# Tiles padded to multiples of 64 bytes, and a planner told of shorter input loads, in a fused recurrence and expert kernel

## The chip, the cores and the metric

The kernel runs on one core of one Trainium2 chip. The metric is the device time of one execution in microseconds (us). The kernel before takes 300.28 us, median of 3 runs (300.28 to 300.85). The change is small against that, so the spread matters here more than usual: in other sessions the same kernel gave single runs from 299.97 to 302.95 us, and every comparison below is with runs of the kernel before from the same session. Ratios are the mean time of one kernel's fast runs over the mean of the other's fast runs in the same rounds, so they are not quite the ratio of the medians that I quote. Brackets behind a ratio hold its 95% interval.

## The reference, cut to what matters

```python
# first stage: gated linear recurrence, B=4, H=8, S=768, D=48
f = 1 / (1 + exp(-f_logit))
for t in range(S):
    state = f[:, :, t, :, None] * state + einsum('bhd,bhe->bhde', k[:, :, t], v[:, :, t])
    y[:, :, t] = einsum('bhd,bhde->bhe', q[:, :, t], state)
# second stage: four experts on x = y as (3072, 384); w1 (4, 384, 1024), w2 (4, 1024, 384)
p = domain_probs / (domain_probs.sum(-1, keepdims=True) + 1e-9)
for e in range(4):
    out += p[:, e:e+1] * (maximum(x @ w1[e], 0) @ w2[e])
```

The recurrence is computed in 6 chunks of 128 steps, as small attention; each chunk's y goes through the four experts. TensorE spends most of its time in the experts.

## The kernel before

Nothing in the program fixes the order of instructions by hand. A planner simulates the engines with a table of costs, and the instructions are then emitted in the order in which its steps began. A load of one batch (128 rows of time, 8 heads of 48 floats: 192 KB in runs of 192 bytes) costs 1.1 us in chunk 0 and 1.05 us later:

```python
def add_load(c, nm, b, n, prio, deps=(), cost=None):
    op = P.add(f"ld {nm}{c}.{b}", {"DMA": cost or (1.05 if c else 1.1) * n}, lambda e: load(c, nm, b, n), prio,
               deps=deps, takes=[(nm, c, b // 2)], lag=2.0)
    ...
for i, x in enumerate("f0 k0 q0 f1 k1 q1 f2 f3 k2 q2 v0 k3 q3 v1 v2 v3".split()):
    add_load(0, x[0], int(x[1]), 1, -1000 + i)
add_load(1, "f", 0, 1, -980, cost=0.1)
...
def load_w(i, e, which, ks, cols):          # expert weights, issued by GpSimd
    ins["w", i] = nc.gpsimd.dma_start(out=w[:, e, ks, cols], in_=r[e][:, ks, cols])
    if i == 0:
        after(ins["w", 0], ins[0, "q", B - 1])      # not before the last q of chunk 0
```

Some tiles are short. They push all that is allocated behind them off a multiple of 64 bytes:

```python
ones = const.tile([T, 1], BF16)             # takes 32 bytes of each partition
...
ident32 = const.tile([NR, NR], FP32)        # NR = 24: 96 bytes
psm = const.tile([T, NR], FP32)             # 96 bytes
shapes = { ... "egs": ([128, NP], FP32), ...}   # 16 bytes
```

Where the plan leaves TensorE waiting before the first expert matmul, the program fills the time with matmuls on a dummy tile (`busy`), 34 of them. One gate step of a later chunk is the chain that will matter: ScalarE reads f (`ex = exp(-f)`, then `gp = ln(1 + ex)`), TensorE sums `gp` along time (line 268), ScalarE takes exponentials of that, GpSimd multiplies q and k by them.

## Time and profile before

| what | kernel before |
|---|---|
| time, median | 300.28 us |
| span in the profile | 298.3 us |
| last q of chunk 0 lands | 16.51 us |
| first / second weight lands | 22.78 / 24.69 us |
| first expert matmul / first on the second weight | 22.83 / 24.73 us |
| from 25.4 us on | TensorE busy without a gap |

The landing times are read from the trace's records of each transfer's last landing. The prediction below shows the page, the stretches and the chain of waits. Three more views are needed for the comparison. Busy time by stretches, in the stretch of the input loads and in the one after the weights' issue; the figures in order are stretch, length, busy time of PE, PEld, DVE, ACT and POOL, granted clock, the DMA engines' share by their packets' time, and GB/s:

```profile
4.00:16.00 12.00, 9.73 (x94) 5.21 (x92) 7.24 (x13) 8.96 (x22) 3.48 (x3) 1.00 1.36 196
...
17.00:18.00 1.00, 0.93 (x10) 0.61 (x8) 1.00 (x3) 0.98 (x4) 1.00 (x2) 1.00 1.35 199
```

The page's row for the queue of all loads that SyncE issues (packets, MB, share of the span that its packets took):

```profile
q1 hardware_dynamic: 129348, 30.14, 60.2%
```

And what TensorE waited for from 14 to 26 us (in total, times, longest):

```profile
PE ps_m L364 <- DMA w_sb<-in_moe_w_dram: 1.1, 2, 0.8
PE ps_t L335 <- DVE vb L228: 0.8, 1, 0.8
PE ps_t L360 <- ACT yb L226: 0.5, 1, 0.5
```

The two waits of line 364 are for the first weight and for the second. The second is the one that counts: after it TensorE never stops again.

### The profile page before, as it was taken

How to read it: one execution, taken by the hardware profiler on the slowest of the kernel's cores; microseconds unless marked ns; L12 is line 12 of the kernel's file. 1: busy time of each engine (PE TensorE's matmuls, PEld its weight loads, DVE VectorE, ACT ScalarE, POOL GpSimd, SP SyncE). 2: the span in 40 equal slices, each digit the busy share in tenths (PEclk: the TensorE clock that was granted, in tenths of full speed). 3: DMA queues.
4: the chain of work that ended last, by engine and by line, in shares of the span. 5: the costliest groups of instructions: out<-in, count | busy, mean ns of one | idle time of the engine just before them, and what ended most of it. 6: DMA issues, size and time to landing. Idle time of an engine off the chain costs nothing.

```text
span 298.3 us, 5572 instructions
## 1 busy us (share of the span) xinstructions
PE 289.1 (97%) x2160; PEld 170.6 (57%) x2160; DVE 126.1 (42%) x247; ACT 176.5 (59%) x325; POOL 105.7 (35%) x179
## 2 busy tenths in 40 slices
PE   6879999999999999999999999999999999999995
PEld 2447555567777776455555555555555555555553
DVE  6657003585675584036375444332532322201223
ACT  4776673857775687877464674555465544465440
POOL 5377401329389159325547553234220000000000
PEclk9999999999999999999999999999999999999999
DMA  8999999997999999999999962102431100200003
GB/s 146 197 186 202 208 208 185 192 186 181 167 165 154 219 156 178 204 185 152 196 168 194 205 115 35 29 0 62 110 69 38 26 2 26 79 2 0 0 0 108
DMA packets 136462, 36.82 MB, mean 123 GB/s; under 512 B 126812, under 2 KB 135644, under 8 KB 136436
## 3 DMA queue, kind: packets, MB, share of 16 engines
q1 hardware_dynamic: 129348, 30.14, 60.2%
q0 software_dynamic: 7088, 6.33, 13.6%
q8 instruction: 17, 0.28, 0.4%
q14 instruction: 9, 0.07, 0.1%
HBM read 31.51 MB, written 4.72 MB: 121 GB/s over the span
## 4 chain that ended last, share of the span: by engine, by line
PE 91%; DMA 4%; SPq 4%; issue 0%; POOL 0%; DVE 0%
PE ps_m L379 42%; PE ps_m L364 42%; SPq L232 3%; DMA w_sb<-in_moe_w_dram 2%; PE ps_t L320 2%; DMA q<-in_q_dram 1%; PE ps_t L335 1%; PE ps_t L331 1%; PE ps_t L341 1%; PE ps_t L268 1%; SPq L247 0%; POOL w_sb L239 0%; PE ps_t L305 0%; DVE o L386 0%; PE ps_t L360 0%
## 5 line engine op out<-in xcount | busy, mean ns | idle before, releaser
L375 ACT ACTIVATE h<-ps_m 128x512 bf16<-128x512 f32 (+1 forms) x192 | 102.5, 538 | 91.1 <-PE ps_m L364 87.5
L364 PE MATMUL ps_m<-xT,w_sb 128*128 128x512 bf16 (+1 forms) x696 | 152.1, 342 | 1.1 <-DMA w_sb<-in_moe_w_dram 1.1
L379 PE MATMUL ps_m<-w_sb,h 128*128 128x384 bf16 (+1 forms) x776 | 151.6, 324 | 0.0
L379 PEld LDWEIGHTS <-h 128*128 128x128 bf16 x776 | 75.1, 98 | 58.6
L386 DVE SCALAR_TENSOR_TENSOR o<-ps_m,pn,o 128x384 f32<-128x384 f32 (+1 forms) x73 | 44.7, 612 | 110.6 <-PE ps_m L379 104.3
L364 PEld LDWEIGHTS <-w_sb 128*128 128x128 bf16 x696 | 65.5, 98 | 43.9 <-DMA w_sb<-in_moe_w_dram 1.5
L296 POOL TENSOR_TENSOR qk<-q,e 128x384 bf16<-128x384 f32 x19 | 22.5, 1191 | 33.9 <-ACT e L288 22.3
L324 DVE TENSOR_TENSOR AT<-ps_t,mask 128x512 bf16<-128x512 f32 x48 | 29.9, 681 | 5.4 <-PE ps_t L320 5.4
L355 POOL TENSOR_TENSOR Sf<-Sf,egs 48x192 f32<-48x192 f32 x40 | 20.1, 503 | 30.8 <-DVE Sf L348 28.7
L288 ACT ACTIVATE e<-ps_t 128x384 f32<-128x384 f32 x48 | 26.6, 668 | 4.0 <-PE ps_t L268 2.9
L373 DVE TENSOR_SCALAR h<-ps_m 128x256 bf16<-128x256 f32 (+1 forms) x40 | 20.0, 510 | 18.9 <-PE ps_m L364 16.6
L296 POOL TENSOR_TENSOR qk<-k,e 128x384 bf16<-128x384 f32 x20 | 20.3, 1018 | 8.4 <-ACT egs L290 4.7
L348 DVE TENSOR_TENSOR Sf<-Sf,ps_t 48x192 f32<-48x192 f32 x40 | 14.0, 350 | 10.9 <-PE ps_t L341 10.2
L239 POOL DMA_DIRECT2D w_sb<-in_moe_w_dram x11 | 9.0, 823 | 21.0 <-DMA k<-in_k_dram 17.6
L356 POOL CAST sb<-Sf 48x192 bf16<-48x192 f32 x40 | 13.6, 340 | 2.6
L388 ACT ACTIVATE o<-ps_m,pn 128x384 f32<-128x384 f32 x22 | 12.8, 581 | 2.8 <-PE ps_m L379 1.7
L228 POOL CAST vb<-v 128x384 bf16<-128x384 f32 x18 | 9.7, 557 | 9.9 <-DMA v<-in_v_dram 6.0
L260 ACT ACTIVATE ex<-f 128x768 f32<-128x768 f32 (+1 forms) x14 | 10.5, 747 | 3.9 <-DMA f<-in_f_logit_dram 3.9
L614 PE MATMUL ps_m<-busy 128*128 128x512 bf16 x34 | 10.9, 424 | 1.5 <-DVE busy L144 1.5
L293 POOL DMA_DIRECT2D egs<-e x16 | 9.0, 565 | 9.4 <-ACT e L288 9.4
L335 PE MATMUL ps_t<-vb,AT 128*128 128x48 bf16 x192 | 11.5, 184 | 0.9 <-DVE vb L228 0.8
L226 ACT CAST yb<-ps_t 128x384 bf16<-128x384 f32 (+1 forms) x16 | 7.6, 472 | 7.5 <-PE ps_t L335 7.3
(54 smaller groups left out, 122.9 us busy)
## 6 DMA issues: line engine op xcount, KB each, us to landing
out_dram<-o SPq DMA_DIRECT2D x23, 192.0 KB, 2.0
w_sb<-in_moe_w_dram POOLq DMA_DIRECT2D x5, 768.0 KB, 18.2
k<-in_k_dram SPq DMA_DIRECT2D x10, 384.0 KB, 5.3
q<-in_q_dram SPq DMA_DIRECT2D x10, 384.0 KB, 6.2
v<-in_v_dram SPq DMA_DIRECT2D x10, 384.0 KB, 6.1
f<-in_f_logit_dram SPq DMA_DIRECT2D x9, 384.0 KB, 5.0
w_sb<-in_moe_w_dram POOLq DMA_DIRECT2D x6, 384.0 KB, 8.7
f<-in_f_logit_dram SPq DMA_DIRECT2D x6, 192.0 KB, 4.5
```

Source lines behind the costliest of these rows:

```text
L288: nc.scalar.activation(out=o, in_=i, func=AF.Exp, scale=1.0 if j else -1.0)
L296: engines[eng].tensor_tensor(out=tl("qk", c, b)[:, j, :, 0:D].rearrange("t (i r) d -> t i r d", r=2), in0=tl("qk"[j], c, b // 2)[:, hh(b), ...
L324: nc.vector.tensor_tensor(out=tl("AT", c, b)[:, r].rearrange("s i t -> s (i t)"), in0=tl("A", c, b, r).rearrange("s i t -> s (i t)"), in1= ...
L335: nc.tensor.matmul(out=y[:, h * D:(h + 1) * D], lhsT=AT[:, r, i, :], rhs=vb[:, h, :], start=(c == 0), stop=True, skip_group_check=True)
L348: nc.vector.tensor_tensor(out=Sf[rows, b], in0=Sf[rows, b], in1=KV[rows, :, r, :], op=ALU.add)
L355: nc.gpsimd.tensor_tensor(out=Sf[rows, b], in0=Sf[rows, b], in1=eg, op=ALU.mult)
L356: nc.gpsimd.tensor_copy(out=nb[rows, b, :, r * D:(r + 1) * D], in_=Sf[rows, b])
L364: nc.tensor.matmul(out=tl("hp", c, e, fc, n0)[:, n0:n1], lhsT=w1_sb[:, e, kk, fc * 128:(fc + 1) * 128], rhs=tl("xT", c)[:, kk, n0:n1], sta ...
L373: nc.vector.tensor_relu(out=dst, in_=src)
L375: nc.scalar.activation(out=dst, in_=src, func=AF.Relu)
L379: nc.tensor.matmul(out=tl("op", c, e, nt, part)[:, cols], lhsT=tl("h", c, e, half_of(c, nt * T))[:, fc, nt * T:(nt + 1) * T], rhs=w2_sb[:, ...
L386: nc.vector.scalar_tensor_tensor(out=o, in0=op, scalar=pe, in1=o, op0=ALU.mult, op1=ALU.add)
```

## The change

Each short tile is made a multiple of 64 bytes (the padding isn't used), so that every tile starts at one; and since loads are expected to become shorter, the planner is told so, by 14% in chunk 0 and 5% later.

```diff
-    ones = const.tile([T, 1], BF16)
+    ones = const.tile([T, 32], BF16, name="ones")[:, 0:1]
-    ident32 = const.tile([NR, NR], FP32)
+    ident32 = const.tile([NR, 32], FP32, name="ident32")[:, 0:NR]
-    psm = const.tile([T, NR], FP32)
+    psm = const.tile([T, 32], FP32, name="psm")[:, 0:NR]
-        "ex": ([T, 2 * H, D], FP32), "egs": ([128, NP], FP32), ...
+        "ex": ([T, 2 * H, D], FP32), "egs": ([128, 16], FP32), ...
 (three uses of egs take [:, 0:NP]: cut)
-        op = P.add(f"ld {nm}{c}.{b}", {"DMA": cost or (1.05 if c else 1.1) * n}, ...
+        op = P.add(f"ld {nm}{c}.{b}", {"DMA": cost or (1.0 if c else 0.95) * n}, ...
```

So there are two changes in one: where the data lie, and the order of the instructions. Padding alone leaves the order on every engine as it was; the costs alone give the order of the changed kernel. Between the two orders, apart from 4 dummies, only five instructions change their engine by the two traces (one relu, one scaling of an output, one copy, and one product each of q and k, which change places).

> **What bounds the kernel now.** I read the page first, then busy time by stretches, then the chain that ended last, then the timeline of the first 27 us. The page:
>
> ```profile
> span 298.3 us, 5572 instructions
> PE 289.1 (97%) x2160; PEld 170.6 (57%) x2160; DVE 126.1 (42%) x247; ACT 176.5 (59%) x325; POOL 105.7 (35%) x179
> PE   6879999999999999999999999999999999999995
> DMA  8999999997999999999999962102431100200003
> L614 PE MATMUL ps_m<-busy 128*128 128x512 bf16 x34 | 10.9, 424 | 1.5 <-DVE busy L144 1.5
> ```
>
> TensorE is busy 97% of the span, but 10.9 us of that are matmuls on a dummy tile (line 614), which the planner puts where it expects TensorE to wait. All of them lie before the first expert matmul, so the first slices are far less full than they look. I then cut the span where the first expert matmul starts and where the dense part begins:
>
> ```profile
> 10.00:22.80 12.80, 10.31 (x128) 6.24 (x128) 8.43 (x16) 9.66 (x22) 8.08 (x10) 1.00 1.32 189
> 22.80:25.40 2.60, 2.32 (x26) 1.89 (x27) 1.59 (x6) 1.39 (x5) 1.57 (x3) 1.00 1.23 201
> 25.40:295.30 269.90, 269.85 (x1976) 159.79 (x1972) 109.91 (x208) 160.21 (x288) 91.67 (x152) 1.00 0.70 118
> ```
>
> The first pair of figures in each row is stretch and length; the next is PE's busy time. From 25.4 to 295.3 us PE has 269.85 of 269.90 us. Is that real work or a stretched wait? The chain of waits shows groups of 3 matmuls of line 364 at 0.65 us and groups of 4 of line 379 at 0.65 us. There are 6 chunks x 4 experts x (8 + 8) such groups = 384, and 384 x 0.65 = 249.6 us; the chain gives these two lines 42% + 42% of 298.3 = about 249 us. So the experts run at the rate of one group's own time, and the middle has nothing to give. What is left is 22.8 us at the front and 3 us at the end. What holds the front:
>
> ```profile
> 10.12 0.52 ACT L260 ACTIVATE ex<-f 128x384 f32<-128x384 f32 x1 [0.42 <-DMA f<-in_f_logit_dram]
> ...
> 15.55 0.56 DVE L296 TENSOR_TENSOR qk<-k,e 128x384 bf16<-128x384 f32 x1 [0.83 <-DMA k<-in_k_dram]
> ...
> 16.80 7.15 POOL L239 DMA_DIRECT2D w_sb<-in_moe_w_dram  x9 [2.42 <-DMA q<-in_q_dram]
> ...
> 20.31 0.51 ACT L226 CAST vb<-v 128x384 bf16<-128x384 f32 x1 [1.11 <-DMA v<-in_v_dram]
> ...
> 22.83 1.16 PE L364 MATMUL ps_m<-xT,w_sb 128*128 128x256 bf16 x9 [0.82 <-DMA w_sb<-in_moe_w_dram]
> ```
>
> The brackets name what each engine sat idle for: loads, all the way. The first weight may be issued only when the last q has landed (16.5 us), and the first expert matmul waits for that weight. The rate of the DMA engines from 3 to 22.8 us sets when the dense part begins.
>
> **What the Trainium skill says.** "DMA: Bandwidth & Descriptors", section Specifications, wants at least 512 B for line rate. The trace agrees: the input loads are 192 B packets (48 floats), and 192 KB land every 1.05 us or so, about 187 GB/s; the weight pieces (2 KB read, 1 KB written per row) land every 1.92 us for 768 KB read, about 410 GB/s. The same page, section Queues, rings and completion order, says each DMA engine goes round its queues packet by packet. The trace agrees: once the weights are issued at 16.8 us, a v load takes 1.88 us from the landing before it in place of 1.05, so loads and the first weight share one rate, and shortening loads brings the weight forward. "SBUF — State Buffer", section Operand start alignment, says only that an operand must start at a multiple of its element size, and that its runs timed nothing: no page there says what a tile's start at a multiple of 32 but not of 64 costs a DMA. For that I need the trace.
>
> **The change part by part.** (1) Alignment. In the built program before, a 2-byte tile that takes 32 bytes (`ones`) moves all that follows to an odd multiple of 32; further small tiles move it again. Of the input tiles that the first chunk loads into (f0, k0, q0, f1, k1, q1, v0, v1), one alone, f1, happens to start at a multiple of 64 (byte 130304); f2, for the first load of chunk 1, doesn't. The change puts every tile at a multiple of 64. So the kernel before holds the experiment already. The trace's landing records, in us from each load's last landing to that of the next, in the order of issue: k 1.14, q 1.07, f 1.03, k 1.06, q 1.02, **f 0.91, f 0.92**, k 1.05, q 1.05, v 1.28 (a small load of probabilities shares it), k 1.05, q 1.05. The two in bold are the two halves of f1. Same size, same shape, same queue, same queue depth: 0.13 us less, 13%. That is also the 14% that the planner is told (1.10 to 0.95). Rows step by 192 B, so from any base at a multiple of 64 they run through the same four places within 256 B; f1's 256 B base should be no better than the new 64 B ones.
>
> (2) What this is worth. Before the first weight lands at 22.78 us, 17 loads land (16 of chunk 0 and the first of chunk 1); 2 are fast already. 15 x 0.13 = **1.95 us**. The last q comes 11 x 0.13 = 1.4 us earlier (about 15.1), and the first weight about 20.8 us. I give weights and stores no gain: their runs are 1 KB and longer, and they are hidden after that.
>
> (3) The planner. The order of instructions, compared engine by engine, shows the same matmuls of real work in another order and 30 dummy matmuls for 34. Dummies lie in the wait, so 4 x 0.42 us are no gain by themselves. The last batch's y matmuls (0.36 us) and its three transposes (0.33) matter: before, y stood ahead of the first expert matmul; now three expert groups stand ahead of it. So when the second weight lands, 1.9 us after the first in either kernel, some 0.33 us more is still to do. That comes off: 1.95 - 0.33 = **1.6 us**.
>
> (4) Can the other engines follow? From 9 to 21 us VectorE has 2.8 us of idle time, of which 0.83 and 1.12 wait for k and v themselves; ScalarE waits 0.61, 0.70 and 1.11. The waits for loads shrink when loads are earlier, and the rest of the chain moves with them. It is tight: VectorE's last two mask products (1.28 us) now end near 20, and y follows; but y no longer stands ahead of the first expert matmul, so a lag of some tenths is covered.
>
> (5) The middle. 4.8% shorter costs for later loads reorder stores, transposes and a few evictions (one relu from DVE to ACT, one first output scaling the other way). PE has work at every moment there; later data earlier saves nothing.
>
> Sum: 300.28 - 1.6 = **298.7 us**; in the profile the span goes from 298.3 to about 296.7.
>
> **The rivals.** *The start becomes bound by VectorE and ScalarE.* For: ScalarE has 4.21 of 5 us busy from 10 to 15, VectorE 3.84. Against: both still name loads as what they wait for. It would halve the gain: 299.5. *Alignment pays beyond the loads, and the new order closes the small gaps of the front too.* For: from 22.8 to 25.4 PE has 0.28 us idle, and weights move too. Against: the second weight remains a wait. It would make 298.0. *The new order opens a hole later.* For: the stretch from 60 to 120 us mixes attention and experts, and a planner with wrong costs can order an engine badly; DMA is 90% busy there. Against: before, PE lost nothing there, with costs no better. A missed wait would cost 1 to 2 us and leave 300 to 301. *The 13% of f1 is an accident of its place in the queue.* Against: the half of f0 loaded two places earlier took 1.03. Then nothing is gained: 300.2.
>
> **Range and chances.** I give the sum about 55%, the engine-bound start 20%, the better case 12%, a hole or no gain 13%. The range 297.6 to 300.0 holds the first three and part of the last. A change of 2% is 6 us, more than a quarter of the whole front; the loads can't give it and the order would have to fail badly to take it. Faster by over 2%: 0.01; within: 0.98; slower: 0.01.
>
> **What would show it.** Right: input loads of chunk 0 land every 0.91 us or so; the weight issue starts at about 15.4 us in place of 16.8; the first line 364 matmul starts at about 20.9 in place of 22.83; PE stays full from some 23.8 us to its end; x30 on line 614. Wrong: load landings still 1.05 apart (alignment isn't the cause); loads fast but the first line 364 waits for an xT copy by ACT or DVE (the start is theirs); or the front is 1.6 us shorter and the span isn't, with PE idle before lines 320, 331 or 364 later (the new order's hole).

## The result, and the profile after

The changed kernel takes **299.87 us** (299.37 to 300.41, 4 runs) against 300.34 us for the kernel before in the same rounds: ratio 0.9981 [0.9959, 1.0003], the same within 2%. The time lies in the forecast range, but the gain is 0.47 us, where 1.6 was forecast. A second session of five rounds found no gain at all (300.17 us, just above that range): 300.17 against 300.20, ratio 0.9999 [0.9986, 1.0012]. What has to be explained is therefore why an alignment that speeds up the loads gives so little.

The page of the changed kernel, the lines that answer to those in the prediction (some 30 matmul records are missing in this trace, so that its counts of PE, and the x28 on line 614, are a little low; the program has 30 dummies):

```profile
span 297.6 us, 5539 instructions
PE 288.0 (97%) x2128; PEld 170.9 (57%) x2156; DVE 126.6 (43%) x248; ACT 175.1 (59%) x325; POOL 104.8 (35%) x178
DMA  7999999967979979999999622102431100200003
L614 PE MATMUL ps_m<-busy 128*128 128x512 bf16 x28 | 10.5, 494 | 1.6 <-DVE busy L144 1.5
```

This is the fastest run (299.37 us), so its span is 0.7 us shorter, more than the medians differ. The input loads became shorter, as forecast. The same two stretches (the first one ends at 15 us, since the loads are done earlier) and the queue:

```profile
4.00:15.00 11.00, 9.83 (x87) 5.36 (x86) 7.03 (x13) 8.17 (x23) 3.00 (x3) 1.00 1.09 217
...
17.00:18.00 1.00, 0.94 (x14) 0.67 (x15) 0.94 (x2) 0.08 (x1) 1.00 (x3) 1.00 0.98 156
```

```profile
q1 hardware_dynamic: 129348, 30.14, 51.7%
```

The same 129,348 packets and 30.14 MB take 51.7% instead of 60.2% of the engines' span, and the loads move at 217 GB/s instead of 196. The last q lands at 15.12 us in place of 16.51. Then the timeline of TensorE at the first and at the second weight:

```profile
21.56 1.16 PE L364 MATMUL ps_m<-xT,w_sb 128*128 128x256 bf16 x9 [1.09 <-DMA w_sb<-in_moe_w_dram]
...
23.52 0.50 PE L364 MATMUL ps_m<-xT,w_sb 128*128 128x256 bf16 x3 [0.27 <-DMA w_sb<-in_moe_w_dram]
```

Before, these two stood at 22.83 and 24.73, so the front is 1.2 to 1.3 us shorter here. But the span is only 0.7 shorter: something is given back later. The chain of waits says where one piece of it lies. Before, the chain ran through TensorE alone in the middle; now it leaves TensorE for a load of f (start, length, what):

```profile
78.98 6.28 DMA f<-in_f_logit_dram
...
85.29 0.85 ACT ex L260
...
86.16 0.85 ACT gp L264
...
87.06 0.48 PE ps_t L268 x2
```

ScalarE's gate of a later chunk waits for its data: `gp` ends at 87.00 us and TensorE's line 268 starts at 87.06. The timeline of the weight loads shows that TensorE had come there before:

```profile
86.67 0.10 PEld L268 LDWEIGHTS <-Ub 128*128 128x128 bf16 x1
...
87.06 0.10 PEld L268 LDWEIGHTS <-Ub 128*128 128x128 bf16 x1 [0.30 <-issue]
```

It stood still between the two for 0.30 us ("issue" means that the profile names no releaser). In the kernel before, the same two loads follow one another (89.01 us, no bracket), since `gp` ended at 88.76, well ahead. This is not the whole loss, but it is a wait that the prediction said could not exist.

### The profile page after: what moved, and what is told of

It is laid out like the page before. It is cut to its first block, busy times and chain, and to the rows that moved or that the text cites. A ratio compares the mean times of both kernels' runs of the same rounds, so it can differ in the third digit from the quotient of the medians.

```text
span 297.6 us, 5539 instructions
## 1 busy us (share of the span) xinstructions
PE 288.0 (97%) x2128; PEld 170.9 (57%) x2156; DVE 126.6 (43%) x248; ACT 175.1 (59%) x325; POOL 104.8 (35%) x178
## 3 DMA queue, kind: packets, MB, share of 16 engines
q1 hardware_dynamic: 129348, 30.14, 51.7%
## 4 chain that ended last, share of the span: by engine, by line
PE 82%; DMA 6%; SPq 5%; POOL 2%; DVE 2%; issue 2%; ACT 1%; POOLq 0%
PE ps_m L379 38%; PE ps_m L364 38%; SPq L232 5%; DMA w_sb<-in_moe_w_dram 2%; DMA f<-in_f_logit_dram 2%; PE ps_t L320 1%; DMA q<-in_q_dram 1%; POOL qk L296 1%; PE ps_t L335 1%; PE ps_t L331 1%; PE ps_t L268 1%; PE ps_t L341 1%; DVE AT L324 1%; POOL Sf L355 1%; SPq L309 0%
## 5 line engine op out<-in xcount | busy, mean ns | idle before, releaser
L296 POOL TENSOR_TENSOR qk<-q,e 128x384 bf16<-128x384 f32 x20 | 23.4, 1174 | 29.4 <-ACT e L288 23.7
L296 POOL TENSOR_TENSOR qk<-k,e 128x384 bf16<-128x384 f32 x19 | 18.9, 999 | 4.9 <-ACT egs L290 2.6
L388 ACT ACTIVATE o<-ps_m,pn 128x384 f32<-128x384 f32 x21 | 12.2, 581 | 1.5 <-PE ps_m L379 0.5
L264 ACT ACTIVATE gp<-ex 128x768 bf16<-128x768 f32 (+1 forms) x14 | 10.5, 751 | 0.4
```

What stands on the lines that cost most here:

```text
L296: engines[eng].tensor_tensor(out=tl("qk", c, b)[:, j, :, 0:D].rearrange("t (i r) d -> t i r d", r=2), in0=tl("qk"[j], c, b // 2)[:, hh(b), ...
```

## The experiments

There were fifteen runs, three of them (e5, e9, e10) of the changed kernel itself. I take them by question, not in the order of the sessions. "In the same rounds" is meant wherever a time of the kernel before stands beside one.

### Which half of the change does what?

**Padding alone** (e1, and e6 in another session): the changed kernel with the old costs.

```diff
-  {"DMA": cost or (1.0 if c else 0.95) * n}
+  {"DMA": cost or (1.05 if c else 1.1) * n}
```

> The aligned tiles with the planner's old load costs, so the order of instructions of the kernel before, unchanged on every engine. Theory (alignment speeds the loads by 0.13 us each, but only the 11 that lie ahead of the last q move the first weight; the retuned order then gives part of it back): loads of chunk 0 land every 0.9 us, last q at about 15.1 us, first weight about 21.5, first expert matmul 21.6, no hole in the middle; 299.1 us. Rival (the new order is needed to use the faster loads): no faster than the kernel before, 300.3. Rival of the prediction (all 15 loads count): 298.4.

Measured: 299.12 us (298.59 to 299.67) against 300.53; ratio 0.9943 [0.9916, 0.997].

> The aligned tiles with the old order (as e1), beside e5. Theory: 1.4 us under the kernel before again, and the second weight lands at 23.5 us (in e1's profile it was late, 24.1, because a load of chunk 1 ran beside the weights). Rival: no better than e5.

Measured: 299.05 us (298.57 to 300.27) against 300.20; ratio 0.9965 [0.9951, 0.9978]. So padding alone gains 1.15 to 1.4 us by the medians. Beside the changed kernel in one session (e6 and e5 below) it is clearly the faster of the two; the ratio of e1, from another session, overlaps that of the first result.

**New costs alone** (e2): the kernel before with the new costs.

```diff
-  {"DMA": cost or (1.05 if c else 1.1) * n}
+  {"DMA": cost or (1.0 if c else 0.95) * n}
```

> The old tiles (at odd multiples of 32 bytes, bar two input tiles) with the planner's new load costs, so the order of the changed kernel. Theory (the order alone gains nothing and opens a wait of 0.3 to 0.4 us near 86 us for a load of f): front about as before or some tenths later, 300.4 to 300.9 us. Rival (the order is what gains): under 300.0.

Measured: 304.36 us (303.74 to 309.21) against 300.53; ratio of the fast runs 1.012 [1.0086, 1.0154]. One of the six runs is slow (309.21); the median of the five fast ones is 304.14, so the new order loses some 3.6 us when the loads stay slow, far over the 300.4 to 300.9 us that I had expected. The profiled run is the slow one, so I take from it only where a wait lies, not what the run lost. The gate chain of the second half of chunk 2 (chunks count from 0) on ScalarE and TensorE (in brackets the idle time before, and its releaser):

```profile
90.56 0.84 ACT L260 ACTIVATE ex<-f 128x768 f32<-128x768 f32 x1 [1.95 <-DMA f<-in_f_logit_dram]
91.44 0.84 ACT L264 ACTIVATE gp<-ex 128x768 bf16<-128x768 f32 x1
```

```profile
92.33 0.48 PE L268 MATMUL ps_t<-gp,Ub 128*128 128x384 bf16 x2 [1.18 <-ACT gp L264]
```

The place is that of the chain shown above for the changed kernel, with the wait grown to 1.18 us. So this order has TensorE come to line 268 when f has only just arrived; with fast loads it nearly makes it, with slow loads it doesn't.

**The rerun of the whole change** (e5, same session as e6):

> The changed kernel once more, beside e6 on the same chip. Theory (alignment gains 1.4 us or more, the new order gives 0.7 or so of it back): 0.4 to 0.8 us under the kernel before, 0.7 or so over e6, with PE waiting for chunk 2's gates near 87 us in the profile again. Rival (the first measurement of the changed kernel was unlucky): as fast as e6.

Measured: 300.17 us (299.85 to 300.62) against 300.20; ratio 0.9999 [0.9986, 1.0012]. With e6 at 299.05 beside it, the new order costs **1.1 us** on padded tiles.

### Is it the destination of the input loads?

e4 is e1 with only the f, k, q and v tiles moved by 32 bytes; all other tiles stay at multiples of 64 (the diff is shortened).

```diff
-  tiles[kind, key] = pool.tile(shape, dt, name=f"{room}{slot}")
+  n = 2 * H * D                                  # for f, k, q, v
+  raw = pool.tile([T, n + 16], dt, name=f"{room}{slot}")
+  tiles[kind, key] = raw[:, 8:8 + n].rearrange("t (h d) -> t h d", d=D)
```

> The kernel of e1 with the tiles of f, k, q and v alone moved 32 bytes off a multiple of 64; weights, transposes, stores and all else stay at multiples of 64. Theory (what matters is where the 192-byte packets of the input loads land): load intervals back to 1.05 us, last q at 16.5, first expert matmul at 22.8, 300.3 us as before. Rival (weights, transposes or compute operands carry part of it): between e1 and the kernel before, 299.5 or so.

Measured: 300.80 us (300.48 to 302.83) against 300.53; ratio 1.0008 [0.9972, 1.0044]. The whole gain is gone. The stretch and the queue of e4:

```profile
4.00:16.00 12.00, 11.01 (x92) 5.99 (x91) 6.90 (x13) 8.96 (x22) 3.48 (x3) 1.00 1.41 188
```

```profile
q1 hardware_dynamic: 129348, 30.14, 59.6%
```

59.6% is the 60.2% of before again, and loads land mostly 1.05 us apart. This settles the first step of the prediction: it is the destination's start, and it is that of the input loads alone. By the packet records, a 192-byte packet took on average 21 ns before, 22 to 23 ns in e4 and 15 to 16 ns after.

### Why is padding worth 1.2 us and not 1.95?

TensorE at the first two weights in e6, and the stretch in which the weights should start:

```profile
20.92 1.16 PE L364 MATMUL ps_m<-xT,w_sb 128*128 128x256 bf16 x9 [0.63 <-DMA w_sb<-in_moe_w_dram]
...
23.54 0.50 PE L364 MATMUL ps_m<-xT,w_sb 128*128 128x256 bf16 x3 [0.97 <-DVE pn L257]
```

```profile
17.00:18.00 1.00, 0.72 (x17) 0.50 (x15) 0.14 (x2) 0.75 (x2) 1.00 (x2) 1.00 0.50 38
```

The first weight came 1.9 us earlier, as forecast (20.87 for 22.78), but that is luck. Before, the first load of chunk 1 (f, 192 KB) landed ahead of the first weight, at 20.87 us; here the weight overtook it, and the load landed at 22.15. Its packets (queue q1) took the DMA engines' time between the two weights (q0); from 20 to 21 us:

```profile
q1 hardware_dynamic: 947, 0.18, 94.5%
q0 software_dynamic: 58, 0.05, 31.8%
```

The second weight came only 1.19 us earlier (23.50 for 24.69), and all 1.19 us that this run gained are there. The bracket of the second TensorE line names VectorE (`pn`), which ended about when the weight landed; a wait for several things is put down to the last one. In e15 below, the same group ran at 23.92, before `pn` had even begun (24.34): it is the weight that it needs.

The row of the stretch shows where the rest was lost, as far as I can follow it: from 17 to 18 us the DMA engines move 38 GB/s, where 199 were moved before. The loads of chunk 0 are done early; the weights, issued by GpSimd from 15.56 us on, aren't there yet to take over. By the packet records the first weight's packets start 1.6 us after its issue in e6 and 2.35 us before; so the packets start 1.96 us earlier (17.19 for 19.15), but in the standstill the rate is lost again, and the 768th weight packet starts only 0.8 us earlier (22.78 for 23.60). GpSimd is busy in all of that us with its DMA instructions (line 239), but so it is before, at 199 GB/s. Nor was there nothing else to move: SyncE began to issue the load of f at 15.08 us, but the issue took 1.86 us in e6, where it took 1.00 before (e6 first, then the kernel before),

```profile
15.08 1.86 SPq L232 DMA_DIRECT2D f<-in_f_logit_dram  x1
```

```profile
15.99 1.00 SPq L232 DMA_DIRECT2D f<-in_f_logit_dram  x1
```

and its packets started at 19.9 us. The four profiles of the changed kernel show the hole more or less deep (156, 146, 54 and 53 GB/s), and the deep holes (these last two, e6, and e1 with 42) go with a long issue of this load (1.86 to 2.51 us; 1.12 and 0.83 us in the first two). What holds the issue up is not shown. Three kernels tried to recover the hole.

**e7**: padding, and the weights released one load earlier.

```diff
-  after(ins["w", 0], ins[0, "q", B - 1])
+  after(ins["w", 0], ins[0, "k", B - 1])
```

> e6 with one wait moved: the first weight may be issued when the last k has landed, not the last q, 0.9 us earlier; the order of instructions is the same on every engine. If the time from the weight's issue to its landing is fixed (some 6.1 us), the first expert matmul comes up to 0.9 us earlier, 298.3. If loads and the first weight share the DMA engines' rate, as the prediction said, the weight gains 0.3 or less and the v loads are later by as much: 299.0 to 299.3.

Measured: 299.07 us (298.78 to 300.43), ratio 0.9974 [0.9957, 0.9992]; e6 in the same session 299.05. Nothing gained: the first weight's issue starts at 14.02, 1.5 us earlier than in e6, but the second weight lands at 23.44, only 0.06 us earlier, while the last v load comes later (19.85 us) and TensorE waits 1.6 us for it by way of `yb`.

**e14**: padding, and the first load of chunk 1 (the last one queued before the weights) moved behind them. **e15**: e14 and e7 together. (The diff is shortened.)

```diff
-  if (c, nm, b) == (1, "f", 1):          # this load waits for the weights
+  if (c, nm, b) == (1, "f", 0):
+  o = next(o for o in done if o.name == "ld f1.0"); done.remove(o)
+  done.insert(next(i for i in range(len(done)) if done[i].name == "ld f1.1"), o)
```

> The aligned tiles with the old order (e1, e6), and the first load of chunk 1 (192 KB, not needed before 50 us) moved behind the weights, to where its second half waits already. If loads and the first weights share the DMA engines' rate: the second weight lands 0.6 to 0.9 us earlier, at about 22.8, ratio to the kernel before 0.993 to 0.994 (e6 had 0.9965). If what holds the second weight is the wait of the weights' own issue: no gain, 0.9965.

> e14 with the first weight issued when the last k has landed instead of the last q (as e7). If the DMA engines run dry between the loads and the weights' first packets, which come 2.4 us after the issue: the gap closes, the second weight lands another 0.5 to 0.9 us earlier, ratio 0.991. If loads and weights share the rate without a gap: as e14, or some tenths worse because v lands later.

Measured: e14 299.55 us (298.74 to 301.35), ratio 0.9963 [0.9935, 0.999]; e15 299.10 us (298.76 to 301.00), ratio 0.9948 [0.9924, 0.9971]; the kernel before 301.08 in a noisier session. Neither can be told from padding alone (two runs of e14, 301.35 and 301.04, and one of e15, 301.00, have a mean clock of 0.994, of which more below). Neither expectation of an earlier second weight came true: it landed at 24.77 us in e14's profile, which is of the run with 301.35 (the trace has sixteen landing records for each transfer; fifteen of this one's came by 23.18), and at 23.88 in e15's, against 23.50 in e6. With the load of f out of the way the two weights are 1.9 us apart again, but both land later than in e6. So the load of f explains their distance, not the shortfall. Shown are its size (some 0.8 us of the forecast 1.95 are missing at the second weight in e6) and that the DMA engines nearly stop there. Why they do stays open: that they wait for GpSimd's work on the weights is argued only, and e7, which starts that work 1.5 us earlier, doesn't bear it out.

### Why does the new order cost a microsecond?

I compared profiles by TensorE's progress: from the trace's weight loads, the time at which the same amount of matmul work (dummies left out) had been issued, less the same for the kernel before. Negative is ahead. The columns are clock times in the kernel before.

| profile | costs | 27 us | 78 us | 90 us | 132 us |
|---|---|---|---|---|---|
| padding alone, e6 | 1.1 / 1.05 | -1.19 | -1.19 | -1.19 | -1.19 |
| padding alone, e1 | 1.1 / 1.05 | -0.61 | -0.44 | -0.44 | -0.44 |
| changed kernel, first | 0.95 / 1.0 | -1.05 | -1.11 | -0.72 | -0.75 |
| changed kernel, e10 | 0.95 / 1.0 | -0.91 | -0.96 | -0.61 | -0.64 |
| changed kernel, e9 | 0.95 / 1.0 | -0.72 | -0.66 | -0.40 | +0.26 |
| changed kernel, e5 | 0.95 / 1.0 | -0.05 | -0.11 | -0.01 | +0.15 |
| e8 | 1.1 / 1.0 | -0.98 | -0.81 | -0.81 | -0.81 |
| e3 | 0.95 / 1.05 | -0.57 | -0.43 | +0.17 | +2.07 |
| e12 | 0.9 / 0.95 | -0.81 | +0.73 | +1.11 | +1.76 |

The old order keeps in the middle all that it has at 27 us, or nearly; the new order gives back 0.2 to 1.0 us there. From 78 to 90 us three of its four profiles lose 0.26 to 0.39 us.

**e9 and e10** are two more looks at the changed kernel, taken since one profile can't show a loss that varies.

> The changed kernel again, for its trace alone (its two traces so far are of one fast run and one with the matmul clock at half rate from 22.3 to 25.7 us, while its usual time, 300.1, has neither). Theory (the new order has PE waits in the middle that come and go with the landing of chunk 2's loads): PE at full clock, first expert matmul near 21.5, then 0.7 to 1 us lost between 60 and 110 us. Rival (the loss is in the front, before 28 us, by clock or waits): nothing lost later.

> The changed kernel once more for its trace, with the same two readings as for the look before it: 0.7 to 1 us lost between 60 and 110 us, or nothing lost after 28 us.

Measured: 300.30 and 299.40 us, both at full clock, though single runs and so of no certain state; the kernel before 301.13 in that session (300.20 to 302.95). The slower one shows ScalarE's gates of three half-chunks (the second of chunk 2 and both of chunk 3) waiting for f:

```profile
85.60 0.84 ACT L260 ACTIVATE ex<-f 128x768 f32<-128x768 f32 x1 [0.75 <-DMA f<-in_f_logit_dram]
...
104.18 0.84 ACT L260 ACTIVATE ex<-f 128x768 f32<-128x768 f32 x1 [1.32 <-DMA f<-in_f_logit_dram]
...
116.73 0.84 ACT L260 ACTIVATE ex<-f 128x768 f32<-128x768 f32 x1 [2.40 <-DMA f<-in_f_logit_dram]
```

In e6 none of the three has a wait; the first:

```profile
85.15 0.83 ACT L260 ACTIVATE ex<-f 128x768 f32<-128x768 f32 x1
```

In e9, TensorE's weight loads stand still for 0.30 us before 108.85 us and for 0.43 before 118.99, a few us behind the second and third wait; e6 has no such holes. The kernel before waits for f too at this gate, for 0.60 us, and its TensorE loses nothing: there, line 268 starts 0.36 us after `gp` has ended (in e6 1.1 us after, in the changed kernel 0.06). So a wait of ScalarE is harmless or not according to how close the order puts its consumer.

**e3 and e8**: padding with one of the two new costs each.

```diff
   {"DMA": cost or (1.05 if c else 0.95) * n}     # e3: new cost in chunk 0 only
   {"DMA": cost or (1.0 if c else 1.1) * n}       # e8: new cost in later chunks only
```

> Aligned tiles, the new cost for the loads of chunk 0 (0.95) and the old cost for all later ones (1.05). Theory (the later costs made the hole near 86 us): front as in the changed kernel, first expert matmul at 21.6, no loss between 80 and 95 us; 299.3, about 0.4 under the changed kernel. Rival (the hole comes from the order of the front, or is chance): as the changed kernel, 299.9.

> Aligned tiles, the old cost for the loads of chunk 0 (1.10) and the new one for later loads (1.00): the other half of the planner's change. Theory (any change of these costs gives another order, and the old one was found by trial, so most others lose): over e6, by 0.5 to 3 us, with a PE wait that e6 lacks. Rival (the new later cost is right for aligned tiles and helps): at or under e6.

Measured: e3 302.22 us (301.58 to 305.80), ratio 1.0063 [1.0019, 1.0106]; e8 299.56 us (298.37 to 300.07), ratio 0.9975 [0.9961, 0.9989]. Not what I had expected of e3. With the later cost alone (e8) the table shows no loss after 78 us, and e8 can't be told from padding alone; with the cost of chunk 0 alone (e3) it shows a larger loss than with both, and at another place: e3's order has a hole of its own, from ScalarE to TensorE (in total, times, longest):

```profile
ACT e L288 <- DMA egs<-e: 3.1, 1, 3.1
```

```profile
PE ps_m L364 <- ACT h L375: 1.8, 1, 1.8
```

ScalarE sits 3.1 us in front of an `e` whose buffer is still being read by the small `egs` transfer, the relu behind it comes late, and TensorE waits 1.8 us for that relu.

**e12**: padding, with costs nearer to the measured 0.93 us (0.9 in chunk 0, 0.95 later).

```diff
+  {"DMA": cost or (0.95 if c else 0.9) * n}
```

> Aligned tiles with load costs nearer to what the aligned loads took in the traces (0.90 for chunk 0, 0.95 later). Rival (the planner's order is the better the truer its costs, and the changed kernel's were still too long): under 299.0. Theory (each cost pair deals another order, and which one fits the chip isn't told by one cost alone): 299.5 to 303.

Measured: 301.88 us (301.25 to 302.10), ratio 1.002 [0.9992, 1.0048] in a session where padding alone was not run; the progress table puts it behind by 1.76 us at 132 us, after 0.81 ahead. ScalarE waited 3.6 us for f from 60 to 115 us. Truer costs don't make a better order. The planner counts a transfer as landed a fixed 2.0 us after its turn ends, whatever else is under way, and orders every engine strictly by that; each set of costs deals another order.

**e13**: the changed kernel, with three loads of f moved ahead of the v load before them.

```diff
+  for o in [o for o in done if o.name in ("ld f2.2", "ld f3.0", "ld f3.2")]:
+      at = done.index(o)
+      to = max(i for i in range(at) if done[i].name.startswith("ld v"))
   ... (a check that no buffer is still in use: cut)
+      done.insert(to, done.pop(at))
```

> The changed kernel with three loads of f (chunks 2 and 3) issued ahead of the load of v that stood before each; all engines but the DMA queue keep their order. Theory (ScalarE's wait for these loads, 0.9 to 2.3 us in the changed kernel's traces and none with the old order, makes the loss of 0.3 to 0.9 us in the middle): no such wait between 60 and 115 us, and 0.3 to 0.8 us less than the changed kernel, a ratio of 0.997 to 0.998 to the kernel before. Rival (the loss in the middle has another cause, or v, now later, takes over): ratio 0.999 to 1.000.

Measured: 302.38 us (301.32 to 303.09) against 301.08; ratio 1.0046 [1.0024, 1.0069]. A miss. ScalarE's waits for f between 60 and 120 us are gone, and others have come, first on GpSimd, then on TensorE (here, and once more for 1.05 us before 116.91):

```profile
POOL vb L228 <- DMA v<-in_v_dram: 2.4, 1, 2.4
```

```profile
97.60 0.40 PE L320 MATMUL ps_t<-QK 48*128 48x128 bf16 x8 [0.79 <-DMA QK<-qk]
98.44 0.40 PE L320 MATMUL ps_t<-QK 48*128 48x128 bf16 x8 [0.45 <-DMA QK<-qk]
```

In this order f, v and the transposes by DMA all arrive just in time; moving one forward makes another late. So the test that I had meant to confirm the waits for f as the cause of the middle's loss didn't: the loss comes with the order, that much is shown; which one of its close calls makes the most of it stays open.

### Is it the clock of TensorE?

e5's profile shows a third part of the loss. TensorE's clock by slices (tenths), and then stretches of 3.4 us (length, busy time of PE, clock, DMA share, GB/s):

```profile
PEclk9997999999999999999999999999999999999999
```

```profile
18.90:22.30 3.40, 1.54 (x14) 1.00 1.20 189
22.30:25.70 3.40, 3.40 (x27) 0.52 1.23 200
```

After a stretch in which TensorE was busy for 1.54 of 3.40 us, the next 3.41 us ran at half clock, and at 27 us this run is only 0.05 us ahead of the kernel before. The Trainium skill, "TensorE: Matmul & The Clock Gate", section "Part 1: The HAM clock gate (the "warmup" mystery)", has the clock fall to half after an idle window of 3413 ns, at a phase that no kernel sets. The length agrees with the trace. The prediction had called the four dropped dummies "no gain by themselves" and never asked whether they keep the clock up.

**e11** puts four dummies in front of the first expert matmul of the changed kernel.

```diff
+  next(o for o in done if o.name.startswith("h 0.")).pad += 4
```

> The changed kernel with 4 more dummy matmuls just ahead of the first expert matmul (34 in all, as the kernel before has), nothing else moved. If the changed kernel loses time because PE stands idle for more than a us before the first weight and its clock is halved for a window: no run under a mean clock of 0.998, and 299.3 or less. If the loss is in the middle: 300.1 as the changed kernel, with or without the dummies.

Measured: 300.30 us (299.51 to 300.81), ratio 0.9966 [0.9939, 0.9993] against a kernel before that was slow that day (301.13); the two looks at the changed kernel beside it gave 299.40 and 300.30. Not distinguishable, so inconclusive as a remedy: no run has a mean clock under 0.998, as the first reading wanted, but the time is that of the second. Its own profile, at full clock, goes from about 1.35 us ahead at 78 us to 0.4 at 132, so this order loses in the middle there too. As the main cause the clock is out: of e5's five runs only one has a mean clock of 0.994, the mark of such a window, the other four are at 1.0, and they take 299.85 to 300.62 us. The window also falls in single runs of the kernel before and of e6 (300.27 us is such a run).

### What beats both kernels

Padding with the old costs: 299.05 us (e6) and 299.12 us (e1), against 300.20 and 300.53 for the kernel before, 300.17 for the changed one. None of the variants of it was better beyond the spread.

## Why the prediction was wrong

By its own steps:

1. **Alignment shortens the input loads by 0.13 us: right in kind, nearly in size.** The intervals in chunk 0 fell from 1.05 to about 0.93 us (the eleven without the small load of probabilities), the last q came 1.4 us earlier, as forecast, and e4 shows that it is those tiles' start. The one fast tile in the kernel before was a fair experiment. A page might have suggested the size as well: the Trainium skill, "DMA: Bandwidth & Descriptors", section "How a descriptor splits into AXI transactions", has the first transaction of a descriptor that does not start at a multiple of 256 bytes begin at the multiple below, in beats of 32 bytes. The page words this for reading; that it holds for writing into a tile is my assumption. For rows 192 bytes apart, an estimate by that rule is 6 + 12 + 10 + 8 = 36 beats for four rows from a start at a multiple of 64, and 7 + 13 + 11 + 9 = 40 from one at 32 beside it: 11% more. The trace has 1.05 for 0.93 us, 13% more; that fits, but no run here looks at beats. The prediction overlooked that section. (The half of f0 that it names against the last rival stands three loads earlier, not two; nothing hangs on it.)
2. **15 x 0.13 = 1.95 us of earlier weights: the term that was mis-sized.** The first weight did come 1.3 to 2.1 us earlier in the four profiles. The sentence that failed is "when the second weight lands, 1.9 us after the first in either kernel": in e6, e9 and e10, where the load of f came between them, it came 2.6 to 3.0 us after (1.95 and 1.89 in the other two profiles of the changed kernel). The second weight, which sets where the dense part begins, came 0.9 to 1.5 us earlier. Padding alone was worth 1.15 to 1.4 us by medians, in place of 1.95. The landings were added up as if weights began the moment that loads ended; in e6, e9 and e10 the DMA engines stood nearly still between them for about 1 us. The reading of the trace that this step leans on was wrong too: the v load with 1.88 us wasn't slowed by the first weight, whose first packet started at 19.15 us, when fifteen of that load's sixteen landing records had come (by 18.52; the last at 19.39). That loads and weights share one rate shows in e6 instead, from 20 to 21 us.
3. **The order gives back 0.33 us: too small.** It gave back 1.1 us (e5 against e6 in one session); from the first result, and so across sessions, 1.15 - 0.47 = 0.7.
4. **The other engines can follow: right.** The first expert matmul waited for its weight in the changed kernel, not for ScalarE or VectorE.
5. **"PE has work at every moment there; later data earlier saves nothing": the step that failed.** The premise held for the old order and was carried over to an order that had never run. That the kernel before lost nothing from 25.4 us on says that its order's slack is enough, not that any order's is. The new order gives back 0.2 to 1.0 us in the middle, and 3.6 us in all where loads are slow (e2). Which wait of the new order makes the most of it stays open (e13).

The right outcome was the rival "the new order opens a hole later", with 300 to 301 us and only part of 13% of the chances; its own argument against itself, "PE lost nothing there, with costs no better", is the same slip as in step 5. Sum with the measured terms: 1.15 to 1.4 us from the padding, less 0.7 to 1.1 us for the order, leaves 0.05 to 0.7 us; measured were 0.47 and 0.03.

## What to carry to other kernels

Where loads consist of short runs, look at the destination's start within 64 bytes: here it was worth some 12% of each load's time, and a short tile far ahead in the pool can spoil it for all. When a planner's costs are retuned together with a real improvement, measure the two apart, since the new order is a new program and a full TensorE under the old order says nothing of it. And follow a gain to the last wait before the dense part (here the second weight), not to the first.

## What the Trainium skill lacked or had wrong

- "SBUF — State Buffer", section Operand start alignment, is where one looks for it, and says of speed only that its runs timed nothing; a rule that would give it, if it holds for writing, stands in the page on DMA (the section named above), without a time and without a word on SBUF destinations. The number that both lack: a destination at a multiple of 32 but not of 64 bytes makes packets of 192 bytes take on average 21 to 23 ns in place of 15 to 16, and loads land 1.05 us apart in place of 0.93 (the changed kernel against before; e4 brings it back).
- "DMA: Bandwidth & Descriptors", section Specifications, gives a first byte by the GpSimd path after about 1 us. Here the first weight's packets started 1.6 us (e6) to 2.35 us (before) after the start of the issue, behind loads still under way, and for about 1 us in between the engines moved only 38 GB/s in e6. I found no page that says how long such a hand-over takes.
- "TensorE: Matmul & The Clock Gate", in the section named above, ties half clock to an idle window of 3413 ns. The length agrees (3.41 us), but the window before it wasn't idle: TensorE was busy for 1.54 of 3.40 us in e5. How little work counts as idle is not in that section's table.
